# Six steps moved to other places in the first five units of a linear-attention and MLP kernel

## The chip, the cores and the metric

The kernel runs on one core of a Trainium2 chip. A time is the device time of one execution in microseconds. Its profiles come from single executions taken by the hardware profiler; a profile's span runs from the first to the last instruction. The engines are called PE (TensorE's matrix products), PEld (its weight loads, which overlap the products), DVE (VectorE), ACT (ScalarE), POOL (GpSimd) and SP (the queue that issues most DMAs).

## The reference

A linear attention with a decaying state gives y, and an MLP with SiLU follows. All data are float32.

```
B, H, S, D = 4, 8, 768, 48
for t in range(S):
    cur = einsum('bhd,bhe->bhde', u * k[t], v[t])
    y[t] = einsum('bhd,bhde->bhe', r[t], state + cur)
    state = w[t][..., None] * state + einsum('bhd,bhe->bhde', k[t], v[t])
x = y as (B*S, H*D)                  # 3072 x 384
h = x @ w_in                         # 384 x 2048
out = (h / (1 + exp(-h))) @ w_out    # 2048 x 384
```

## The kernel before

The work is cut into twelve units, 0 to 11. A unit is 128 tokens of two batches (`units` lists six stretches of tokens times two pairs of batches), so units 0 and 1 have no earlier state. A unit goes through these stages.

- `turn` brings w, k and r into a layout with the channels in the partitions (`tw`, `tk`, `tr`). For units 0 and 1 that is a product on PE with copies by ACT (L356, L357, L360), for the later ones six transposes by DVE (L336).
- Scores between tokens are made in seven levels l, doubling the block of tokens each time. `product` multiplies decays (POOL, L384). `start_keys` (L505), `odd_ones` (L495), `odd_keys` (L459) and `grow_keys` (L489, POOL) prepare the keys of a level; `grow_queries` (L471) and `prepare` (L593, L595) prepare the queries. `score_products` (L525) are the products, and `keep_masked` (L535) copies what the mask keeps into `score`. From unit 2 on two levels are computed in one `burst`.
- `bonus`, `bonus_sum` (L413, L417), `bonus_spread` and `bonus_write` (L448) put in the token's own term with u.
- `y_state` (L650) and `y` (L663) make y, copied by ACT to `yt` (L667). `turn_k` makes the keys for the state: for units 0 and 1 copies by ACT (L633) out of products of `turn_apart` (L626), later eight transposes on PE (L637) and two copies by ACT (L638). `update` (L677, L682, L691, L693) makes the new state.
- x for the MLP: `dense_x` (L701, copy L703) for units 0 and 1, DMAs (`move_x`) later.
- `up(i, m)`, m from 0 to 7: products with w_in (L754) and the SiLU by ACT (L760).
- Unit 0's output comes from `down` (L773, copied at L777). From unit 1 on it comes from seven products of half the size, `quarter(i, 0)` to `quarter(i, 6)` (L817), called q0 to q6 here. They work on sums of the activations (`sums`, L799, DVE) and of the weights (`weight_sums`, L791, DVE, four calls in the whole kernel). Their results leave PSUM by an ACT copy for q0 (L824) and by DVE additions for the others (L826). The PSUM tile `p_o` of the seven products has two buffers.

The weights come in sixteen pieces, eight of w_in and eight of w_out, and are rounded during units 0 to 2. For piece i, `head_weight` is two ACT instructions (L194, the upper part of the words, and L195), `tail_weight` one (L201, into the single PSUM tile `p_w`), `join_weight` two DVE instructions (L212, L213) and, where the staging place is used again, the DMA of a later piece; `add_weight` is a POOL addition (L225). `piece(i)` is this chain with the head and tail of piece i+1 in it.

Every engine runs its instructions in the order in which the code issues them, and that order is written by hand: the lists given to `do(...)` for units 0 to 2, and from unit 3 on `mix(i)`, which gives groups of attention steps, with `ROOM`, which says how many MLP steps (`quarter` of unit i-2, `up` of unit i-1) follow each group. `b12` and `b21` are quarters of w_out; the fourth call of `weight_sums` puts b21 - t2 in the place of b12, which q5 reads:

```
out, one, two = ((t1, b12, b11), (t2, b22, t1), (t3, b22, b12), (b12, b21, t2))[which]
left, right = ((g(0, 0), b11), (g(0, 1), b21), (s(1), t2), (s(2), t3), (s(0), t1), (g(1, 1), b12), (s(3), b22))[which]
```

Of the kernel before, what the change touches and what calls it, by code (L numbers as in the profile page):

```python
# [9 lines left out]
BF16 = mybir.dt.bfloat16  # L10
I8 = mybir.dt.int8
I32 = mybir.dt.int32
U16 = mybir.dt.uint16
U32 = mybir.dt.uint32
AF = mybir.ActivationFunctionType
# [23 lines left out]
def kernel(  # L39
# [11 lines left out]
    nc = tc.nc  # L51
# [4 lines left out]
    NL = 7  # L56
# [11 lines left out]
    NTOK = 2  # L68
# [94 lines left out]
    def staged(i):  # L163
        place = PLACES[i] - NOWN
        if place < 0:
            return own[:, PLACES[i]]
        return w_out_sb[:, 4 * place:4 * place + 4, :].rearrange("p a d -> p (a d)").bitcast(U32)
# [17 lines left out]
    shift = const.tile([128, 1], F32, name="shift")  # L185
    temps = const.tile([128, 3, 2, PW], U32, name="temps")

    def head_weight(i):
        if not rounded:
            return  # L190
        head = temps[:, 0, i % 2]

        upper = temps[:, 1, i % 2].bitcast(BF16)[:, 0:PW]
        nc.scalar.activation(out=upper, in_=staged(i).bitcast(BF16)[:, 3::4], func=AF.Abs)  # L194
        nc.scalar.activation(out=head, in_=upper.bitcast(U16), func=AF.Relu, scale=8.0 * 2.0 ** 16, bias=shift)  # L195

    def tail_weight(i):
        if not rounded:
# [60 lines left out]
    parts = sorted({(ch // 128, ch // (2 * D)) for ch in range(DM)})  # L259
# [457 lines left out]
    def both(fn, i, *args):  # L717
        return [(fn, i, b, *args) for b in range(NB)]

    def block_loads(i):  # L720
        return [(load_blocks, i, name, g) for name in "wkr" for g in range(4)]

    def mix(i):

        groups = [[*both(turn, i, "w"), (product, i, 0)],
                  [*both(turn, i, "k"), *both(turn, i, "r"), (odd_ones, i), (start_levels, i), (prepare_keys, i, 1)],
                  [(prepare, i, 1), *[(product, i, l) for l in range(1, NL)]],
                  [(burst, i, 1), (keep_level, i, 1)], [(keep_level, i, 2), (go_on, i, 2)],
                  [(prepare, i, 3), (reverse_v, i), (bonus, i, 0)],
                  [(burst, i, 3), (keep_level, i, 3), (bonus_sum, i, 0), (bonus, i, 1), (bonus, i, 2)],  # L730
                  [(keep_level, i, 4), (go_on, i, 4)],
                  [(prepare, i, 5), (bonus_sum, i, 1)] + ([(load_rk, i + 1)] if i + 1 < len(units) else []),
                  [(burst, i, 5), (keep_level, i, 5)], [(keep_level, i, 6), (go_on, i, 6), (bonus_spread, i), (bonus_write, i)],
                  both(turn_k, i), [*both(y_state, i), *both(y, i), *both(update, i), (move_x, i)]]

        loads = block_loads(i + NSLOT) if i + NSLOT < len(units) else []
        if i + 1 < len(units):
            loads.insert(len(loads) // 2, (load_values, i + 1))
        behind = groups[2:]
        for at, group in enumerate(behind):  # L740
            group += loads[at * len(loads) // len(behind):(at + 1) * len(loads) // len(behind)]
        return groups
# [89 lines left out]
    def ups(i):  # L832

        steps = [[(up, i, m)] for m in range(FC // 2)]
        for m in range(FH // 2 - 1):

            steps[FH // 2 + 1 + m].append((sums, i, m))
        steps[-1].append((sums, i, FH // 2 - 1))
        return steps

    def downs(i):
        return [[(quarter, i, x)] for x in range(7)]

    def do(*steps):
        for fn, *args in steps:
            fn(*args)
# [7 lines left out]
    def back(fn, i, *args):  # L854
        return both(fn, i, *args)[::-1]


    do((make_spread,), (beat, 16), *both(turn, 0, "k"), (odd_ones, 0), (bonus, 0, 0), (bonus, 0, 1), *both(turn, 0, "r"),
       (bonus_sum, 0, 0), (clear_dense,), (clear_state,), *back(turn, 0, "w"), (bonus, 0, 2), (start_keys, 0, nc.vector, True),
       (start_keys, 0, nc.vector, False), (grow_queries, 0, 0), (product, 0, 0, nc.vector), (odd_keys, 0, 1), (grow_keys, 0, 1),  # L860
       (make_dense,), (beat, 16))

    blocks = block_loads(2)
    others = {1: [(clear, 0), (beat, 6)], 2: [(turn, 1, 0, "r"), (head_weight, 0), (beat, 2)],
              3: [(turn, 1, 1, "r"), (head_weight, 1), (beat, 2)], 4: [(turn, 1, 1, "w"), (reverse_v, 0)],
              5: [(bonus_spread, 0), (bonus_write, 0), (turn, 1, 0, "w")], 6: [*both(turn_in, 1, "k"), *blocks[0:4], (tail_weight, 0)]}
    between = {4: [(bonus_sum, 0, 1)]}
    for l in range(1, NL):
        do((scores, 0, l, *between.get(l, ())), *[(grow_keys, 0, l + 1)] * (l + 1 < NL), *others[l])

    do((bonus, 1, 0), (bonus, 1, 1), (bonus, 1, 2), *both(y, 0), (turn_apart, 0), (join_weight, 0), (add_weight,),
       *blocks[4:8], (product, 1, 0), (tail_weight, 1), (turn_k, 0, 0), (join_weight, 1), (dense_x, 0, 0), (turn_k, 0, 1),
       *both(turn, 1, "k"), (dense_x, 0, 1), (grow_queries, 1, 0), (odd_ones, 1), (tail_weight, 2), (head_weight, 2),
       *blocks[8:12], (start_keys, 1, nc.gpsimd, True), (add_weight,), (up, 0, 0), (join_weight, 2),
       (start_keys, 1, nc.gpsimd, False), (add_weight,), (tail_weight, 3), (odd_keys, 1, 1), (head_weight, 3), (grow_keys, 1, 1),
       (scores, 1, 1, (join_weight, 3)), (add_weight,), (up, 0, 1), (tail_weight, 4), (grow_keys, 1, 2), (head_weight, 4),
# [3 lines left out]
    others = {1: [], 2: [(bonus_sum, 1, 0), (bonus_sum, 1, 1), (load_rk, 2), *both(update, 0)],  # L880
              3: [(bonus_spread, 1), (reverse_v, 1), (clear, 1), (load_values, 2)]}
# [5 lines left out]
    for m in range(1, 4):  # L887
# [1 line left out]
    do((head_weight, 8), (join_weight, 7), (scores, 1, 5), (grow_keys, 1, 6), (add_weight,), (tail_weight, 8), (up, 0, 6),  # L889
       (bonus_write, 1))  # L890

    do((scores, 1, NL - 1), (head_weight, 9), (join_weight, 8), (add_weight,), (up, 0, 7), *both(y, 1), (turn_apart, 1),
       (tail_weight, 9), *both(turn_k, 1), *both(dense_x, 1), (piece, 9), *both(update, 1), (up, 1, 0), *both(turn, 2, "w"))
    blocks = block_loads(3)

    others = {0: [(up, 1, 1), (down, 0, 0, 0), *both(turn, 2, "k"), (product, 2, 0), (product, 2, 1)],
              1: [(up, 1, 2), *both(turn, 2, "r"), *[(product, 2, l) for l in range(2, NL)], *blocks[0:3]],
              2: [(down, 0, 0, 1), (odd_ones, 2), (start_keys, 2, nc.gpsimd, True), (grow_queries, 2, 0), *blocks[3:6]],
              3: [(up, 1, 3), (start_keys, 2, nc.gpsimd, False), (reverse_v, 2), *blocks[6:9]], 4: [(level, 2, 1), (up, 1, 4), *blocks[9:12]],
              5: [(down, 0, 0, 2), (up, 1, 5), (weight_sums, 0)]}  # L900
    for m in range(6):
# [4 lines left out]
    blocks = block_loads(4)  # L906
# [2 lines left out]
    do(blocks[2], (burst, 2, 3), (keep_level, 2, 3), (keep_level, 2, 4), (go_on, 2, 4), (prepare, 2, 5), (bonus, 2, 1),  # L909
       (bonus, 2, 2), (down, 0, 1, 2), (bonus_sum, 2, 1), (load_rk, 3), (sums, 1, 1), *blocks[3:7], (down, 0, 1, 3))  # L910
    do((burst, 2, 5), (keep_level, 2, 5), (keep_level, 2, 6), (go_on, 2, 6), (up, 1, 6), (bonus_spread, 2), (bonus_write, 2),
       (load_values, 3), (weight_sums, 2), (up, 1, 7), (sums, 1, 2))
    do(*both(turn_k, 2), (sums, 1, 3), *both(y_state, 2), *both(y, 2), (weight_sums, 3), *both(update, 2), (move_x, 2),
       *blocks[7:])

    ROOM = 1, 1, 2, 1, 1, 1, 1, 1, 2, 1, 2, 1, 0
    for i in range(3, len(units)):
        steps = downs(i - 2) + ups(i - 1)
        groups = mix(i)
        for group, room in zip(groups, ROOM):  # L920
            do(*group)
            for step in steps[:room]:
                do(*step)
            steps = steps[room:]
# [32 lines left out]
```

## Time and profile before

| what | value |
|---|---|
| median of 6 runs | 652.44 us (651.54 to 653.82) |
| the profiled execution | 651.54 us, span 649.7 us |
| busy, PE / DVE / POOL / ACT | 639.9 / 431.6 / 280.9 / 203.0 us |
| time from a unit to the next from unit 3 on | 50.94 us |
| mean granted clock of TensorE | 1.00 |

A line of a list of instructions gives the start and the duration in us, the engine, the line of the code, the operation, what is written and read with shapes, and in brackets the engine's idle time ahead of it with what ended it. A line of the list of waits gives the instruction that waited, the one it waited for, the total in us, how often, and the longest.

### The profile page before, as it was taken

Reading aid. Unit: us, or ns where it says so; the run is one execution under the profiler, and the core shown is the slowest. Engines: PE = TensorE matmul, PEld = TensorE weight load, DVE = VectorE, ACT = ScalarE, POOL = GpSimd, SP = SyncE. Lnnn points to the kernel's source line nnn. Section 1 sums busy time; section 2 is a strip of 40 time slices with the busy share of each in tenths; the row PEclk is TensorE's granted clock in tenths of the full one; section 3 lists DMA queues with packets and bytes.
Section 4 is the critical chain, followed back from the end, with each engine's and each line's share of the span. In section 5 each row is a group of like instructions: output and inputs, shape, how many; then the busy total and the mean of one; then the engine's idle time right before and its main releaser. Section 6 shows DMA issues by size and latency. Waiting matters only on the chain.

```text
span 649.7 us, 12886 instructions
## 1 busy us (share of the span) xinstructions
PE 639.9 (98%) x4878; PEld 579.0 (89%) x4878; DVE 431.6 (66%) x737; ACT 203.0 (31%) x408; POOL 280.9 (43%) x356
## 2 busy tenths in 40 slices
PE   8999999989999999999999999999999999999998
PEld 7878876889899899899899899899899989989997
DVE  6979789887487576585595676576676765752031
ACT  6797971211221321331331232231232232131120
POOL 6898398455055254334425416416416505510000
PEclk9999999999999999999999999999999999999999
DMA  9956954444534414514513513433431022000000
GB/s 227 275 93 174 272 127 51 88 79 57 108 53 75 87 32 65 97 30 67 96 29 56 109 25 48 95 48 52 76 71 38 26 50 49 26 3 25 25 0 25
DMA packets 201134, 49.21 MB, mean 76 GB/s; under 512 B 188912, under 2 KB 195952, under 8 KB 201072
## 3 DMA queue, kind: packets, MB, share of 16 engines
q1 hardware_dynamic: 199488, 47.79, 36.0%
q10 hardware_dynamic: 1584, 0.59, 0.4%
q8 instruction: 39, 0.64, 0.4%
q14 instruction: 23, 0.19, 0.1%
HBM read 39.52 MB, written 4.72 MB: 68 GB/s over the span
## 4 chain that ended last, share of the span: by engine, by line
PE 88%; POOL 3%; ACT 3%; DMA 2%; SPq 2%; DVE 1%; issue 1%; DVEq 0%; POOLq 0%; ACTq 0%
PE p_h L754 35%; PE p_o L817 30%; PE p_sc L525 6%; PE p_m L525 4%; PE p_m L663 3%; PE p_m L650 2%; PE p_m L773 2%; PE p_m L348 1%; PE p_m L637 1%; SPq L106 1%; POOL tk L489 1%; PE p_sc L677 1%; DMA w_out_sb<-in_moe_w_in_dram 1%; DMA w_out_sb<-in_moe_w_out_dram 1%; ACT temps L194 1%
## 5 line engine op out<-in xcount | busy, mean ns | idle before, releaser
L754 PE MATMUL p_h<-xt,w_in_sb 128*128 128x256 f32 x1152 | 258.2, 382 | 0.7 <-ACT tk L357 0.7
L754 PEld LDWEIGHTS p_h<-xt,w_in_sb 128*128 128x128 f32 x1152 | 215.8, 190 | 32.6 <-POOL tk L505 0.9
L760 ACT ACTIVATE gt<-p_h 128x512 f32<-128x512 f32 x93 | 55.5, 597 | 225.2 <-PE p_h L754 225.1
L489 POOL TENSOR_TENSOR tk<-tk,tw 128x256 f32<-128x256 f32 x144 | 99.2, 713 | 22.4 <-ACT tk L459 16.1
L535 DVE COPY_PREDICATED score<-mask,p_sc 128x512 f32<-128x512 int8 x78 | 64.1, 884 | 60.5 <-PE p_sc L525 60.2
L817 PE MATMUL p_o<-own,temps 128*128 128x192 f32 x528 | 90.3, 328 | 2.5 <-DVE temps L826 2.5
L817 PE MATMUL p_o<-w_out_sb,gt 128*128 128x192 f32 x528 | 90.4, 328 | 0.0
L817 PEld LDWEIGHTS p_o<-own,temps 128*128 128x128 f32 x528 | 85.8, 190 | 3.9 <-DVE temps L826 2.8
L817 PEld LDWEIGHTS p_o<-w_out_sb,gt 128*128 128x128 f32 x528 | 85.9, 190 | 0.9 <-issue 0.4
L682 POOL TENSOR_TENSOR state<-state,tw 128x512 f32<-128x512 f32 x16 | 19.1, 1213 | 119.0 <-PE p_m L650 119.0
L384 POOL TENSOR_TENSOR tw<-tw 128x256 f32<-128x256 f32 (+6 forms) x83 | 38.0, 457 | 56.7 <-DVE tw L336 52.8
L799 DVE TENSOR_TENSOR temps<-gt 128x256 f32<-128x256 f32 x88 | 44.3, 503 | 21.5 <-ACT gt L760 21.5
L459 ACT COPY tk<-tk 128x256 f32<-128x256 f32 x60 | 24.6, 410 | 85.1 <-PE p_sc L525 38.1
L525 PEld LDWEIGHTS p_sc<-tr,tk 48*128 48x128 f32 x640 | 39.2, 186 | 12.7 <-issue 9.8
L471 DVE TENSOR_TENSOR tr<-tr,tw 128x512 f32<-128x512 f32 x53 | 47.3, 893 | 2.6 <-PE p_sc L525 0.8
L525 PE MATMUL p_sc<-tr,tk 48*128 48x128 f32 x640 | 47.1, 285 | 1.3 <-POOL tk L489 0.6
L406 POOL TENSOR_TENSOR ruk<-tokens_rk 128x768 f32<-128x768 f32 x10 | 18.6, 1860 | 68.7 <-DVE own_sums L413 68.7
L593 DVE TENSOR_TENSOR tr<-tr,tw 128x512 f32<-128x512 f32 x29 | 36.4, 1257 | 0.4
L535 DVE COPY_PREDICATED score<-mask,p_m 128x512 f32<-128x512 int8 x54 | 35.4, 705 | 0.0
L826 DVE TENSOR_TENSOR partial<-p_o,partial 128x192 f32<-128x192 f32 x33 | 11.7, 353 | 34.7 <-PE p_o L817 34.7
L505 POOL TENSOR_TENSOR tk<-tk,tw 128x128 f32<-128x128 f32 x44 | 32.5, 774 | 2.3 <-ACT tk L495 1.7
L817 PE MATMUL p_o<-w_out_sb,temps 128*128 128x192 f32 x176 | 30.4, 326 | 0.0
(144 smaller groups left out, 741.8 us busy)
## 6 DMA issues: line engine op xcount, KB each, us to landing
w_out_sb<-in_moe_w_in_dram SPq DMA_DIRECT2D x6, 768.0 KB, 7.3
tokens_rk<-in_r_dram SPq DMA_DIRECT2D x20, 192.0 KB, 3.3
tokens_rk<-in_k_dram SPq DMA_DIRECT2D x20, 192.0 KB, 3.7
w_out_sb<-in_moe_w_out_dram SPq DMA_DIRECT2D x4, 768.0 KB, 5.8
own<-in_moe_w_out_dram SPq DMA_DIRECT2D x4, 768.0 KB, 6.4
xt<-yt SPq DMA_DIRECT2D x60, 48.0 KB, 2.0
raw<-in_w_dram SPq DMA_DIRECT2D x80, 32.0 KB, 2.1
raw<-in_k_dram SPq DMA_DIRECT2D x80, 32.0 KB, 2.2
```

Source lines behind the costliest of these rows:

```text
L384: engine.tensor_tensor(out=up, in0=t[:, :, 0::2], in1=t[:, :, 1::2], op=ALU.mult)
L459: nc.scalar.copy(out=keys(i, X[(l + 1) % 2] * L + c, [4 * c, blocks], [c, 2], [1, c]), in_=keys(i, NP * L + c, [4 * c, blocks], [NP * L + ...
L471: nc.vector.tensor_tensor(out=odd, in0=odd, in1=tw[i][l][:, :, 0::2][:, :, :, None].to_broadcast([128, Q, L >> (l + 1), c]), op=ALU.mult)
L489: nc.gpsimd.tensor_tensor(out=out, in0=have, in1=odd_products(i, l, b, *blocks), op=ALU.mult)
L505: engine.tensor_tensor(out=keys(i, X[1] * L + 3 * b, [4, n], [1, 1]) if own else have, in0=have, in1=odd_products(i, 0, b, [4, n], skip=2 ...
L525: nc.tensor.matmul(bass.AP(tensor=s_p.tensor, offset=s_p.offset, ap=[s_p.ap[0], [apart * L // 2, 2], [1, L // 2]]), lhsT=tk[i][rows, X[l % ...
L535: nc.vector.copy_predicated(out=dst, mask=masks[l][:, :, None].to_broadcast([128, NB, NP, ni, c]), data=sc[e].rearrange("p (b q) (i c) -> ...
L593: nc.vector.tensor_tensor(out=new[:, :, :, 1, :], in0=old[:, :, :, 1, :], in1=tw[i][l][:, :, 0::2][:, :, :, None].to_broadcast([128, Q, L ...
L754: nc.tensor.matmul(p_h[:, a, :], lhsT=w_in_sb[:, c, f * 128:(f + 1) * 128], rhs=xt[i][:, c, :], start=(c == 0), stop=(c == KC - 1))
L760: nc.scalar.activation(out=gt[i, m], in_=p_h, func=AF.Silu)
L799: nc.vector.tensor_tensor(out=out, in0=one, in1=two, op=op)
L817: nc.tensor.matmul(p, lhsT=left(f), rhs=right[:, f, :], start=(f == 0), stop=(f == FH - 1))
```

## The change

Six steps are issued at another place; no instruction is added or taken out.

1. `bonus_sum(0, 1)` goes from level 4 of unit 0's scores to before `start_keys` of unit 0.
2. The key copies `turn_k(0, b)` go behind the turned keys of unit 1, `odd_ones(1)` and `tail_weight(2)`.
3. `head_weight(9)` goes from before the last `up` of unit 0 to unit 1's `dense_x`: its first instruction between the two halves, its second behind them. `tail_weight(10)` now precedes `head_weight(10)`.
4. `turn_k(2, b)` goes before the last `up` of unit 1.
5. `weight_sums(3)` goes from the end of unit 2 to the fifth group of unit 3, behind `keep_level(3, 1)`.
6. In `mix` the second group is divided: q1 with its addition now follows the transposes, and `start_levels` and `prepare_keys` come after it. This holds for units 3 to 11.

```diff
-    def head_weight(i):
+    def head_weight(i, parts=range(2)):
...
-        nc.scalar.activation(out=upper, in_=staged(i).bitcast(BF16)[:, 3::4], func=AF.Abs)
-        nc.scalar.activation(out=head, in_=upper.bitcast(U16), func=AF.Relu, scale=8.0 * 2.0 ** 16, bias=shift)
+        if 0 in parts:
+            nc.scalar.activation(out=upper, in_=staged(i).bitcast(BF16)[:, 3::4], func=AF.Abs)
+        if 1 in parts:
+            nc.scalar.activation(out=head, in_=upper.bitcast(U16), func=AF.Relu, scale=8.0 * 2.0 ** 16, bias=shift)
...
-                  [*both(turn, i, "k"), *both(turn, i, "r"), (odd_ones, i), (start_levels, i), (prepare_keys, i, 1)],
+                  [*both(turn, i, "k"), *both(turn, i, "r"), (odd_ones, i)], [(start_levels, i), (prepare_keys, i, 1)],
...
-        behind = groups[2:]
+        behind = groups[3:]
...
-       (bonus_sum, 0, 0), (clear_dense,), (clear_state,), *back(turn, 0, "w"), (bonus, 0, 2), (start_keys, 0, nc.vector, True),
+       (bonus_sum, 0, 0), (clear_dense,), (clear_state,), *back(turn, 0, "w"), (bonus, 0, 2), (bonus_sum, 0, 1), (start_keys, 0, nc.vector, True),
...
-    between = {4: [(bonus_sum, 0, 1)]}
...
-        do((scores, 0, l, *between.get(l, ())), *[(grow_keys, 0, l + 1)] * (l + 1 < NL), *others[l])
+        do((scores, 0, l), *[(grow_keys, 0, l + 1)] * (l + 1 < NL), *others[l])
...
-       *blocks[4:8], (product, 1, 0), (tail_weight, 1), (turn_k, 0, 0), (join_weight, 1), (dense_x, 0, 0), (turn_k, 0, 1),
-       *both(turn, 1, "k"), (dense_x, 0, 1), (grow_queries, 1, 0), (odd_ones, 1), (tail_weight, 2), (head_weight, 2),
+       *blocks[4:8], (product, 1, 0), (tail_weight, 1), (turn, 1, 0, "k"), (join_weight, 1), (dense_x, 0, 0), (turn, 1, 1, "k"),
+       (dense_x, 0, 1), (grow_queries, 1, 0), (odd_ones, 1), (tail_weight, 2), *both(turn_k, 0), (head_weight, 2),
...
-    do((scores, 1, NL - 1), (head_weight, 9), (join_weight, 8), (add_weight,), (up, 0, 7), *both(y, 1), (turn_apart, 1),
-       (tail_weight, 9), *both(turn_k, 1), *both(dense_x, 1), (piece, 9), *both(update, 1), (up, 1, 0), *both(turn, 2, "w"))
+    do((scores, 1, NL - 1), (join_weight, 8), (add_weight,), (up, 0, 7), *both(y, 1), (turn_apart, 1),
+       (tail_weight, 9), *both(turn_k, 1), (dense_x, 1, 0), (head_weight, 9, [0]), (dense_x, 1, 1), (head_weight, 9, [1]),
+       (join_weight, 9), (add_weight,), (tail_weight, 10), (head_weight, 10), *both(update, 1), (up, 1, 0), *both(turn, 2, "w"))
...
-       (load_values, 3), (weight_sums, 2), (up, 1, 7), (sums, 1, 2))
-    do(*both(turn_k, 2), (sums, 1, 3), *both(y_state, 2), *both(y, 2), (weight_sums, 3), *both(update, 2), (move_x, 2),
+       (load_values, 3), *both(turn_k, 2), (weight_sums, 2), (up, 1, 7), (sums, 1, 2))
+    do((sums, 1, 3), *both(y_state, 2), *both(y, 2), *both(update, 2), (move_x, 2),
...
-    ROOM = 1, 1, 2, 1, 1, 1, 1, 1, 2, 1, 2, 1, 0
+    ROOM = 1, 1, 0, 2, 1, 1, 1, 1, 1, 2, 1, 2, 1, 0
...
+        if i == NTOK + 1:
+
+            groups[4].append((weight_sums, 3))
```

## The prediction

> **What bounds the kernel now.** I read the page first (busy shares, chain), then TensorE's list of waits, then the timeline around the longest wait, then a later unit as a standard.
>
> The page's busy shares:
>
> ```profile
> PE 639.9 (98%) x4878; PEld 579.0 (89%) x4878; DVE 431.6 (66%) x737; ACT 203.0 (31%) x408; POOL 280.9 (43%) x356
> ```
>
> TensorE is the bound: it is without work for only 9.8 us of 649.7. The chain gives it 88% of the span, and the granted clock is 1.00 in every stage, so no clock is to be won. A move on another engine pays only where it ends a TensorE wait. These are its waits that lie near the moved steps (who waits, for whom: us in total, times, longest):
>
> ```profile
> PE p_o L817 <- DVE temps L826: 2.5, 1, 2.5
> ...
> PE p_h L754 <- ACT tk L357: 0.7, 1, 0.7
> ...
> PE p_sc L525 <- DVE score L535: 0.6, 1, 0.6
> PE p_m L650 <- ACT kq L638: 0.3, 1, 0.3
> PE p_m L701 <- ACT yt L667: 0.2, 1, 0.2
> ```
>
> They are all before 140 us; later TensorE is gapless up to its last product. The timeline of all engines round the first of them (start, duration, engine, line):
>
> ```profile
> 131.79 1.75 DVE L791 TENSOR_TENSOR w_out_sb<-w_out_sb,own 128x1536 f32<-128x1536 f32 x1
> ...
> 133.46 1.11 DVE L691 TENSOR_TENSOR state<-p_sc,state 48x384 f32<-48x384 f32 x2
> ...
> 134.57 2.76 PE L817 MATMUL p_o<-own,temps 128*128 128x192 f32 x16
> 134.59 1.30 DVE L336 STREAM_TRANSPOSE tw<-raw 128x512 f32<-128x512 f32 x2
> ...
> 136.97 3.00 POOL L505 TENSOR_TENSOR tk<-tk,tw 128x128 f32<-128x128 f32 x4
> ...
> 138.30 1.14 DVE L471 TENSOR_TENSOR tr<-tr,tw 128x512 f32<-128x512 f32 x1
> 139.47 0.36 DVE L826 TENSOR_TENSOR temps<-p_o,partial 128x192 f32<-128x192 f32 x1
> ...
> 139.88 2.87 PE L817 MATMUL p_o<-own,temps 128*128 128x192 f32 x16 [2.55 <-DVE temps L826]
> ...
> 140.52 1.44 POOL L489 TENSOR_TENSOR tk<-tk,tw 128x256 f32<-128x256 f32 x2 [0.55 <-ACT tk L459]
> ...
> 142.68 1.18 PE L525 MATMUL p_sc<-tr,tk 48*128 48x128 f32 x16
> ...
> 143.89 2.46 DVE L535 COPY_PREDICATED score<-mask,p_sc 128x512 f32<-128x512 int8 x2 [0.75 <-PE p_sc L525]
> ...
> 144.68 2.87 PE L817 MATMUL p_o<-own,temps 128*128 128x192 f32 x16
> ```
>
> Call the seven products of a unit's output q0 to q6. They alternate between two PSUM buffers, so q3 (139.88) needs q1's buffer. q1 ends at about 134.7, but L826, which empties it, stands on VectorE behind L791, L691, six L336 and L471 and runs at 139.47. q2 ends at 137.33: hence 2.55 us. The same place one unit later:
>
> ```profile
> 188.32 5.36 PE L817 MATMUL p_o<-own,temps 128*128 128x192 f32 x32
> 189.07 1.16 DVE L471 TENSOR_TENSOR tr<-tr,tw 128x512 f32<-128x512 f32 x1
> 190.26 0.36 DVE L826 TENSOR_TENSOR temps<-p_o,partial 128x192 f32<-128x192 f32 x1
> ...
> 193.62 0.98 PEld L525 LDWEIGHTS p_sc<-tr,tk 48*128 48x128 f32 x16 [0.23 <-POOL tw L384]
> ```
>
> There q2 and q3 run as one group of 32: no subtraction of weights stands in the way, and nothing is to be won.
>
> **The change part by part.** No moved step issues a DMA, and the order on SP and on POOL stays as it is. The joins that trigger weight loads (pieces 12 to 15) keep their places on SP.
>
> *Unit 0's sums.* Two reductions (1.00 us for both at 23.00) go to the end of L408 (10.29), in front of L505. VectorE stands idle there for 1.16 us, waiting for ScalarE's tw copy, which ends at 11.41. They end near 11.25: 0 us, with 0.15 to spare; L505 is on the chain, so what they exceed counts in full. At 23 us nothing is won, since TensorE has no gap from 16.06 to 31. Bounds: 0 to +0.2.
>
> *Unit 0's key copies.* Four L633 (two of 0.54 us each time) leave 33.38 and 34.62 for a place behind the third L201. The turned keys of unit 1 and L201 come 0.9 us sooner, but TensorE's next wait (0.74 at 36.30) is in truth for the second xt copy on VectorE (35.59 to 36.15, just ahead of it), which starts when dense_x ends: it stays. Behind it ScalarE loses some 0.2 us of idle time in front of L703, so L194, L760 and the next L201 (40.04) come 0.13 sooner. L201, L212, L213, L471, L535 is the chain to the wait of 0.62 at 46.65. I take 0.1 (bounds 0 to 0.3; L201 also needs L760, which needs the product ending at 39.1). The copies hold both p_sc buffers until about 37.6, and scores need them at 39.05: covered by 1.4 us.
>
> *Upper parts of weights 9.* L194 and L195 (0.93 + 0.94 at 68.09) stood before L760 and the yt copies. Without them yt starts when its product is done (69.5, not 70.57) and dense_x follows turn_apart at once: 0.2 gained. L194 now lies between the two xt copies: from about 72.9 to 73.8, while dense_x's second half ends at 73.8. The second xt ends at 74.4, and TensorE is at the state's products until 74.6: covered by 0.2. Bounds: +0.4 to -0.2. L195 moves from 69.11 to some 74.3, POOL's addition from 74.61 to 75.4. POOL's next addition is at 79.68 and piece 9 is first read near 80.9: hidden. L760 of unit 1 may slip by some tenths, which ScalarE's idle 1.39 us at 85.59 takes up.
>
> *Turned keys of unit 2.* Eight L637 go between two products of `up`. ScalarE's copies (1.07) then run beside the second (2.7 us), so L650 does not wait: 0.3 gained. The copies come ahead of L760, whose output is read by the last L799 at 130: hidden.
>
> *Fourth subtraction and grouping.* Without L791, L691 starts at 131.5 instead of 133.46, counting the 0.6 us won before. Six transposes and L826 follow; from L691 to the end of the transposes is 4.84 in the trace, so L826 ends at 136.7. q2 ends at 137.33 - 0.6 = 136.7: all 2.55 go. What is late next? The burst at 139.5 needs the keys: 6.0 us after the first transposes (L384 1.04, four L505 3.00, ScalarE 0.55, L489 1.44), so 139.7, and its second half needs them at 140.6. Covered by 0.9.
>
> The new wait is q5, which reads the weights that L791 now makes behind L535. L535 starts 1.2 after the burst, at 140.7, lasts 2.4, and L791 starts at 143.1. q4 ends at 144.2. With 1.75 us L791 ends at 144.85 and q5 waits 0.7. Queued behind L791 on VectorE are q4's two L826 (needed by q6, 147.6), L535 and L471: covered by 1.5.
>
> *A rule against it.* The other long subtraction with POOL's key products beside it took 2.22 us, the three without 1.75. Two L799 beside POOL's L682 took 1.26 and 1.15 instead of 0.41. The Trainium skill (SBUF — State Buffer, Who interferes with whom) says that a VectorE instruction with two SBUF inputs and a GpSimd instruction that reads SBUF exclude each other, and the second waits for the first to finish. At 131.79 POOL was idle; at 143.1 its four L489 (2.62) are running, then L404 (1.00). By the lowest row the loss at q5 is 0.7, by the 2.22 row 1.15, by the rule with a whole L404 in front 1.7. I take 0.9: the L489 are nearly done by then.
>
> *Units 4 to 11.* L826 goes ahead of L471. q1 is done when VectorE gets there (188.5 against 189.0), so L471 starts 0.36 later. L593, which follows, ends at 191.3 and the burst is at 193.62: covered by 2. 0 us.
>
> The other rule weighed is how to measure the gap. TensorE's matmul row says 2.55, its weight-load row 2.8. The skill (Perfetto Trace Analysis, Identifying the Most-Contended Engine) calls matmul busy time a poor measure of headroom and prefers weight-load time. The sum would be 0.25 better; I keep the smaller, since the products start by the first.
>
> **Sum:** 0 + 0.1 + 0.2 + 0.3 + 2.55 - 0.9 + 0 = 2.25 us gained. The profiled execution took 651.54 (span 649.7), the lowest of six; it becomes 649.3, the span 647.4. Off the median of 652.44: 650.2.
>
> **The rivals.**
> 1. *The exclusion at q5 is longer, or the head's tenths do not come.* With q5 at 1.7 and the head at 0: 2.55 + 0.3 - 1.7 = 1.15, so 651.3. For it: L404 follows just there.
> 2. *The burst waits for the keys instead.* POOL's L505 run beside the transposes and L471. If the 6.0 us become 8, the burst's second half comes 1.1 late: 651.3. With 3.2 us or more nothing is left: 652.4. Against it: unit 4 shows the same spacing (L384 186.74 to L489 191.33).
> 3. *Slower: L826 ahead of L471 in units 4 to 11.* If the burst hung on L471, the 0.36 would be paid in eight units: 2.9 lost against 2.25 won, 653.1. It decides from 0.28 per unit; at 0.44, which takes a wait for q1 as well, the kernel is slower beyond the measurement. For it: the weight load there ends an idle 0.23. Against: the 2 us of cover.
> 4. *The wait is not L826's.* q3 also reads sums and weights of VectorE, but these end at 131.9. Then 652 or so.
>
> **How the numbers follow.** The forecast (gain 1.5 to 2.6) 0.72; rival 1 0.12; rival 2 0.08; rival 3 0.05; rival 4 0.03. A measurement of this kernel can tell about 0.2%, 1.3 us, from no change. Faster by more: the forecast, half of rival 1 and a little of 2: 0.80. Slower: 0.05, rounded up to 0.06 for what I do not see; the rest, 0.14, is within. The forecast alone is 649.8 to 650.9; the runs scatter by 2.3, so a median is good to half a microsecond. Reaching to rivals 1 and 2: 649.2 to 651.6.
>
> **What would show it.** Right: q2 and q3 as one L817 group of 32 near 134; one wait of 0.6 to 1.2 for L791 at q5 near 145; L650 and L701 gone from the list of waits; L791 near 143 with 1.75 to 2.2 us; TensorE's idle time down from 9.8 to about 7.5; units from 150 us on alike and 50.94 apart. Wrong: a q5 wait over 2, a burst near 140 waiting for POOL, L505 of unit 0 after 11.6, or gaps in units 4 to 11.

## The result, and the profile after

| | before | after |
|---|---|---|
| median | 653.17 us (37 runs, 650.59 to 658.76) | 650.25 us (16 runs, 648.71 to 651.34) |
| profiled execution / its span | 651.54 / 649.7 us | 650.52 / 648.7 us |
| TensorE idle in the span | 9.8 us | 648.7 - 639.4 = 9.3 us |

The ratio of the times is 0.9952, with a 95% interval from 0.9936 to 0.9968: about 3.1 us faster (2.1 to 4.2), where 2.25 was forecast. Line numbers of after are those of before plus 2 (the subtraction is L793, the addition that empties q1 is L828). The page's busy shares:

```profile
PE 639.4 (99%) x4878; PEld 578.3 (89%) x4878; DVE 433.4 (67%) x737; ACT 203.6 (31%) x408; POOL 282.6 (44%) x356
```

TensorE has the same work, and its granted clock is 1.00 again. Its list of waits in after (who waits, for whom: us in total, times, longest), without those below 0.25:

```profile
PE p_m L854 <- POOL ident masks.py:199: 1.4, 1, 1.4
PE p_m L665 <- ACT score L556: 0.9, 1, 0.9
PE p_o L819 <- DVE w_out_sb L793: 0.8, 1, 0.8
PE p_h L756 <- POOL tk L507: 0.7, 1, 0.7
PE p_sc L527 <- POOL tk L491: 0.6, 1, 0.6
PE p_m L350 <- DMA raw<-in_k_dram: 0.4, 1, 0.4
PE p_h L527 <- DVE tr L473: 0.4, 1, 0.4
PE p_o L819 <- DVE temps L828: 0.4, 1, 0.4
PE p_h L756 <- ACT gt L762: 0.3, 1, 0.3
```

Gone are the 2.5 us for q1's addition (0.4 is left), the 0.6 for `score`, and those of L650 and L701. New are 0.8 for the moved subtraction, as forecast, and four that the prediction did not have: 0.9 for L556, 0.4 for L473, 0.3 for L762, and 0.4 for the DMA of an input block at 5 us, ahead of every moved step. The timeline of all engines around q3 and q5 (start, duration, engine, line, and in brackets the idle time ahead with its releaser):

```profile
134.15 2.76 PE L819 MATMUL p_o<-own,temps 128*128 128x192 f32 x16
...
136.88 0.36 DVE L828 TENSOR_TENSOR temps<-p_o,partial 128x192 f32<-128x192 f32 x1
137.15 0.87 DVE L473 TENSOR_TENSOR tr<-tr,tw 128x512 f32<-128x512 f32 x1
137.29 2.87 PE L819 MATMUL p_o<-own,temps 128*128 128x192 f32 x16 [0.38 <-DVE temps L828]
...
141.30 2.46 DVE L537 COPY_PREDICATED score<-mask,p_sc 128x512 f32<-128x512 int8 x2 [0.75 <-PE p_sc L527]
...
142.83 4.01 POOL L491 TENSOR_TENSOR tk<-tk,tw 128x256 f32<-128x256 f32 x4
143.56 2.17 DVE L793 TENSOR_TENSOR w_out_sb<-w_out_sb,own 128x1536 f32<-128x1536 f32 x1
...
145.79 2.87 PE L819 MATMUL p_o<-w_out_sb,gt 128*128 128x192 f32 x16 [0.84 <-DVE w_out_sb L793]
```

q3 starts at 137.29 instead of 139.88, q5 waits 0.84, and the unit's next burst starts at 151.19 instead of 152.67. Followed along the span, after leads before by 0.31 us at unit 2's state products (L652 at 124.37, L650 at 124.68), by 2.59 at q3, by 1.48 at that burst, and by only 0.93 at unit 4's q2 (187.39 against 188.32). From 152 us to the end TensorE has one gap, and it is where the last half microsecond goes. The row's gap is 0.28, but the starts show the whole cost: from the transposes (L639) to the state products (L652) after takes 177.60 - 173.59 = 4.01 us, before 178.54 - 175.07 = 3.47.

```profile
169.84 2.44 SPq L425 DMA_DIRECT2D diag<-own_sums  x4
172.29 0.20 ACT L441 COPY both_b<-diag 128x16 f32<-128x16 f32 x1 [3.08 <-DMA diag<-own_sums]
...
173.53 0.84 ACT L443 COPY both_b<-diag 32x16 f32<-32x16 f32 x4 [1.03 <-DMA diag<-own_sums]
...
174.27 1.06 ACT L762 ACTIVATE gt<-p_h 128x512 f32<-128x512 f32 x2
174.91 2.86 PE L756 MATMUL p_h<-xt,w_in_sb 128*128 128x256 f32 x12 [0.28 <-ACT gt L762]
```

The four DMAs of the diagonal stand in SP's queue behind the block loads of a later unit. In before they were issued at 169.44, when the products were 1.48 us later, and TensorE waited for nothing. In after they come at 169.84 although TensorE is early; ScalarE stands at L441 and L443 for them, with the SiLU (L762) queued behind, and TensorE waits for that. The next experiments test this.

### The profile page after: what moved, and what is told of

The parts are those of the page before. It is cut to its first block, busy times and chain, and to the rows that moved or that the text cites. A ratio compares the mean times of both kernels' runs of the same rounds, so it can differ in the third digit from the quotient of the medians.

```text
span 648.7 us, 12887 instructions
## 1 busy us (share of the span) xinstructions
PE 639.4 (99%) x4878; PEld 578.3 (89%) x4878; DVE 433.4 (67%) x737; ACT 203.6 (31%) x408; POOL 282.6 (44%) x356
## 4 chain that ended last, share of the span: by engine, by line
PE 87%; DVE 4%; DMA 3%; SPq 3%; ACT 1%; issue 1%; POOL 0%; DVEq 0%; ACTq 0%; POOLq 0%
PE p_h L756 33%; PE p_o L819 31%; PE p_sc L527 6%; PE p_m L527 3%; PE p_m L775 3%; PE p_m L665 3%; PE p_m L652 3%; SPq L106 2%; PE p_m L639 1%; DVE score L537 1%; DMA u_bc<-in_u_dram 1%; PE p_m L350 1%; DMA w_out_sb<-in_moe_w_in_dram 1%; PE p_sc L679 1%; DMA w_out_sb<-in_moe_w_out_dram 1%
## 5 line engine op out<-in xcount | busy, mean ns | idle before, releaser
L762 ACT ACTIVATE gt<-p_h 128x512 f32<-128x512 f32 x93 | 55.4, 596 | 223.6 <-PE p_h L756 223.4
L491 POOL TENSOR_TENSOR tk<-tk,tw 128x256 f32<-128x256 f32 x144 | 103.3, 741 | 21.7 <-ACT tk L461 15.1
L684 POOL TENSOR_TENSOR state<-state,tw 128x512 f32<-128x512 f32 x16 | 19.3, 1227 | 119.0 <-PE p_m L652 119.0
L801 DVE TENSOR_TENSOR temps<-gt 128x256 f32<-128x256 f32 x88 | 44.3, 503 | 21.5 <-ACT gt L762 21.5
L473 DVE TENSOR_TENSOR tr<-tr,tw 128x512 f32<-128x512 f32 x53 | 46.1, 870 | 3.3 <-POOL tk L491 1.1
L408 POOL TENSOR_TENSOR ruk<-tokens_rk 128x768 f32<-128x768 f32 x10 | 18.6, 1859 | 66.7 <-DVE own_sums L415 66.7
L595 DVE TENSOR_TENSOR tr<-tr,tw 128x512 f32<-128x512 f32 x29 | 39.3, 1354 | 1.3
L597 ACT COPY tr<-tr 128x512 f32<-128x512 f32 x29 | 18.4, 635 | 37.2 <-DVE tr L473 36.4
L507 POOL TENSOR_TENSOR tk<-tk,tw 128x128 f32<-128x128 f32 x44 | 29.3, 701 | 1.7 <-ACT tk L497 1.7
## 6 DMA issues: line engine op xcount, KB each, us to landing
tokens_rk<-in_r_dram SPq DMA_DIRECT2D x20, 192.0 KB, 3.4
tokens_rk<-in_k_dram SPq DMA_DIRECT2D x20, 192.0 KB, 3.8
```

What stands on the lines that cost most here:

```text
L473: nc.vector.tensor_tensor(out=odd, in0=odd, in1=tw[i][l][:, :, 0::2][:, :, :, None].to_broadcast([128, Q, L >> (l + 1), c]), op=ALU.mult)
L491: nc.gpsimd.tensor_tensor(out=out, in0=have, in1=odd_products(i, l, b, *blocks), op=ALU.mult)
L507: engine.tensor_tensor(out=keys(i, X[1] * L + 3 * b, [4, n], [1, 1]) if own else have, in0=have, in1=odd_products(i, 0, b, [4, n], skip=2 ...
L595: nc.vector.tensor_tensor(out=new[:, :, :, 1, :], in0=old[:, :, :, 1, :], in1=tw[i][l][:, :, 0::2][:, :, :, None].to_broadcast([128, Q, L ...
L762: nc.scalar.activation(out=gt[i, m], in_=p_h, func=AF.Silu)
L801: nc.vector.tensor_tensor(out=out, in0=one, in1=two, op=op)
```

## The experiments

Times are medians; each ratio is to runs of before on the same chip (653.15 in the first group, 653.84 in the second). The last group was run once each (650.00, 653.52, 653.89 and 650.49 us in the order below, before beside them 654.05) and is read by its traces alone.

**First group: which part does what near q3.**

Parts 5 and 6 alone, put on before:

```diff
-    do(*both(turn_k, 2), (sums, 1, 3), *both(y_state, 2), *both(y, 2), (weight_sums, 3), *both(update, 2), (move_x, 2),
+    do(*both(turn_k, 2), (sums, 1, 3), *both(y_state, 2), *both(y, 2), *both(update, 2), (move_x, 2),
...
+        if i == NTOK + 1:
+            groups[4].append((weight_sums, 3))
```

with the second group of `mix` divided as in the change.

> Before with the moves of the fourth subtraction and the grouping alone (parts 5 and 6). Theory: the unit 3 exchange carries the gain, 2.55 us of wait at q3 against some 0.9 at q5: 1.5 to 1.9 us faster than before in time, and in the trace q3's wait falls to under 0.6 while q5 gets one of 0.7 to 1.2. The wait of 0.62 for L535 near 46.65 and that of 0.29 at L650 stay. Rival (the gain sits in the head: the tail of the other four moves makes most of the measured 0.48%): under 0.7 us faster.

Measured: 651.54, ratio 0.9976 (0.9953 to 0.9998), about 1.6 us (0.1 to 3.1). q2 and q3 run as one group of 32, and q5 pays what it pays in after:

```profile
135.39 5.36 PE L817 MATMUL p_o<-own,temps 128*128 128x192 f32 x32
...
144.16 2.17 DVE L791 TENSOR_TENSOR w_out_sb<-w_out_sb,own 128x1536 f32<-128x1536 f32 x1
...
146.38 2.87 PE L817 MATMUL p_o<-w_out_sb,gt 128*128 128x192 f32 x16 [0.83 <-DVE w_out_sb L791]
```

So these two parts end q3's wait without the others. The waits of before at 46.7 (0.62) and 125.5 (0.29) are still there, and that of L701 is 0.89. TensorE also waits 0.66 for the SiLU at 175.9: part of the gain is given back there too.

Parts 1 to 4 alone:

```diff
-    ROOM = 1, 1, 0, 2, 1, 1, 1, 1, 1, 2, 1, 2, 1, 0
+    ROOM = 1, 1, 2, 1, 1, 1, 1, 1, 2, 1, 2, 1, 0
...
-            groups[4].append((weight_sums, 3))
```

with the fourth subtraction and `mix` as in before.

> Before with parts 1 to 4 alone (sums, key copies, weights 9, turned keys). Theory: 0.3 at L650 and 0.6 at the scores near 46, and 0.2 at dense_x: 0.6 to 1.2 us faster than before; the wait of 2.5 at q3 stays as it is. Rival: these moves are worth 1.5 us or more because they also take up the late landing of the weights near 64 us. The forecast had 0.6 for the four.

Measured: 652.74, ratio 0.9988 (0.9963 to 1.0014), not told from no change. The waits at 46, L652 and L703 are gone, but one line shows where their gain went:

```profile
138.96 0.36 DVE L828 TENSOR_TENSOR temps<-p_o,partial 128x192 f32<-128x192 f32 x1
139.37 4.55 PE L819 MATMUL p_o<-own,temps 128*128 128x192 f32 x16 [3.22 <-DVE temps L828]
```

q3's wait has grown from 2.55 to 3.22, where it was expected to stay. The group ahead of q3 starts 1.19 us earlier than in before (133.38 against 134.57), VectorE's addition and q3 only 0.51 earlier (139.37 against 139.88): more than half of what the head won ends in this wait.

The second line holds something else. q3's sixteen products take 4.55 us, where they took 2.87 in before. TensorE's granted clock was halved behind the wait. By stretches of 1 us (the stretch, its length, TensorE's busy time and products, the granted clock, the DMA share, GB/s):

```profile
138.00:139.00 1.00, 0.00 (x0) 1.00 0.17 43
...
141.00:142.00 1.00, 1.00 (x4) 0.50 0.27 73
...
144.00:145.00 1.00, 1.00 (x20) 1.00 0.42 51
```

This one stretch costs 4.55 - 2.87 = 1.7 us. What it does to the medians is told at the end of this group.

After with the division of the group undone (part 6), and after with the subtraction put back (part 5):

```diff
-                  [*both(turn, i, "k"), *both(turn, i, "r"), (odd_ones, i)], [(start_levels, i), (prepare_keys, i, 1)],
+                  [*both(turn, i, "k"), *both(turn, i, "r"), (odd_ones, i), (start_levels, i), (prepare_keys, i, 1)],
```

> After, with the division of the second group taken back (part 6 undone), so that L826 of q1 stands behind L471 again in all units. Theory: q3 of unit 3 waits 1.2 to 1.6 us instead of 0.38, q5's wait is the same as before within 0.3, units 4 to 11 stay without a wait: about 1.0 us slower than after. Rival (the grouping is not needed once the subtraction is gone): no difference from after.

```diff
-    do((sums, 1, 3), *both(y_state, 2), *both(y, 2), *both(update, 2), (move_x, 2),
+    do((sums, 1, 3), *both(y_state, 2), *both(y, 2), (weight_sums, 3), *both(update, 2), (move_x, 2),
...
-            groups[4].append((weight_sums, 3))
```

> After, with the fourth subtraction back at the end of unit 2 (part 5 undone). Theory: L826 of q1 runs 1.7 us later, q3 waits 1.8 to 2.2 us, q5 waits for nothing: about 0.9 us slower than after. Rival (the grouping alone does it, the subtraction only brings a new wait): as fast as after or faster, q3's wait under 0.8.

Measured: 651.77, ratio 0.9974 (0.9951 to 0.9996), and 651.16, ratio 0.9962 (0.9932 to 0.9992). With the head's parts in, the four traces give q3's wait for every combination:

| q3 waits (us) | group whole | group divided |
|---|---|---|
| subtraction in unit 2 | 3.22 | 2.03 |
| subtraction in unit 3 | 1.65 | 0.38 |

The division takes 1.19 or 1.27, the move of the subtraction 1.57 or 1.65, each whatever the other does. The division takes L471 out of the way: 1.15 us in the trace of the undivided group (L473 at 137.60, ahead of L828 at 138.78). There unit 4's q3 waits 0.70 at 192.0 as well, where no wait was expected. Without the moved subtraction there is no wait at q5 and none at 175. Its median is the lowest of this group's four, but the intervals overlap.

**What the waits do to the clock.** The trace with the subtraction put back shows the same halving behind q3's wait of 2.03 (0.50 from 139 to 141, and again 4.55 us for q3's products), and the trace of the third group with the turned keys put back shows it behind a wait of 1.92 for L556. Not every long wait brings it: the profile of before has 2.55 us at q3 and a clock of 1.00. One halved stretch lowers the mean clock of an execution to 0.997 (1.7 of 650 us is 0.26%), so the clocks on record show how often it happens:

| first group | executions at 0.997 or lower |
|---|---|
| before | 18 of 35 |
| parts 1 to 4 alone | 9 of 12 |
| after with the subtraction put back | 4 of 10 |
| parts 5 and 6 alone | 0 of 12 |
| after with the group undivided | 0 of 10 |

After itself has none in 17. In the second group before has 11 of 16, and the four kernels tested there, all with the subtraction in unit 3, none in 29. So moving the subtraction also ends most of the halvings, which the prediction had ruled out as a gain because the one profile of before showed a clock of 1.00. The 17 executions of before at 1.00 in the first group have a median of 652.41, against 653.15 for all 35. By that mark some 0.7 us of a gain measured against before is clock, and of the 1.6 us of parts 5 and 6 alone 0.9 remain. These are estimates between medians. No trace of before with a lowered clock was kept, so it is not shown that its halvings lie at q3 too.

**Second group: what is late next, and can it be taken away.** The subtraction ahead of both copies of `keep_level(3, 1)` instead of behind them:

```diff
-            groups[4].append((weight_sums, 3))
+            groups[4].insert(1, (weight_sums, 3))
```

> After, with the fourth subtraction one step earlier on VectorE: behind the burst of unit 3 but ahead of keep_level(3, 1). Theory (q5's wait is only the place of the subtraction): it runs near 140.6 while VectorE would wait for the burst, ends near 142.5, and q5's wait of 0.84 is gone. But the diagonal's DMA of unit 3 lands at an hour of its own, near 172, so the wait for L762 near 175 grows by what q5 gives: less than 0.4 us faster than after. Rival (the wait near 175 follows TensorE): 0.8 faster, no larger wait near 175.

Measured: 651.15, ratio 0.9953 (0.9932 to 0.9974). q5's wait is gone, and the ratio is no better than after's 0.9952. From q3 to the next burst TensorE takes 12.80 us instead of 13.90, so 1.1 are won at q5. ScalarE and TensorE 30 us later:

```profile
170.34 2.44 SPq L425 DMA_DIRECT2D diag<-own_sums  x4
172.78 0.20 ACT L441 COPY both_b<-diag 128x16 f32<-128x16 f32 x1 [4.19 <-DMA diag<-own_sums]
...
175.39 2.86 PE L756 MATMUL p_h<-xt,w_in_sb 128*128 128x256 f32 x12 [1.39 <-ACT gt L762]
```

The wait for the SiLU is 1.39 instead of 0.28, and the way from L639 to L652 takes 5.12 us instead of 4.01: the 1.1 won at q5 are given back at the diagonal's DMAs. (This run is 0.5 us later than after's throughout, by a wait of 1.41 instead of 0.92 for L556 at 69, of which below; 175.39 against 174.91 is just that.) If that is so, the same kernel must gain once SP is free at that time. Hence after with the block loads of unit 3 (and of it alone) from the eleventh group on, so that the diagonal goes first:

```diff
-        behind = groups[3:]
+        behind = groups[10:] if i == NTOK + 1 else groups[3:]
```

> After, with unit 3's block loads (for unit 5) moved on SP behind the diagonal's DMAs: in unit 3 alone they follow the groups from the tenth on. Theory (the wait near 175 is SP's: the diagonal's issues stand behind the loads): the diagonal is issued near 160 and not 169.8, ScalarE no longer waits for it, the wait of 0.28 near 175 is gone and TensorE there follows at once: 0.3 to 0.6 us faster than after. Rival (the wait near 175 is an accident of one profile, or the diagonal waits for VectorE's sums): no difference from after, diagonal issued near 170.

Measured: 649.55 (6 runs, 649.13 to 650.51), ratio 0.9937 (0.9913 to 0.9961), by the ratios 1.0 us better than after, where 0.3 to 0.6 were expected; the intervals overlap. The diagonal's DMAs are issued at 158.43, ScalarE's copies wait for nothing, and TensorE has no gap there:

```profile
168.26 0.20 ACT L441 COPY both_b<-diag 128x16 f32<-128x16 f32 x1
168.47 0.84 ACT L443 COPY both_b<-diag 32x16 f32<-32x16 f32 x4
...
173.62 2.75 PE L756 MATMUL p_h<-xt,w_in_sb 128*128 128x256 f32 x12
```

Both edits together:

> After, with both: the subtraction ahead of keep_level(3, 1) and unit 3's block loads behind the diagonal's DMAs. Theory: q5's wait and the wait near 175 are both gone and nothing gives the gain back: 1.1 to 1.5 us faster than after. Rival (the gain is given back at another wait in unit 3 or 4): under 0.6 us faster, with a new wait on TensorE in the list.

Measured: 648.71 (6 runs, 647.87 to 649.49), ratio 0.9922 (0.9898 to 0.9946), 2.0 us better than after where 1.1 to 1.5 were expected. Neither q5 nor 175 waits; what is left, besides waits that before has too, is 0.38 at q3 and 1.03 for L556. So the give-back is shown from both sides: the subtraction's earlier place alone brings no measurable gain, and with SP's loads later the median falls by 0.84 with it. The intervals of these two overlap; the waits in the traces are the firmer evidence.

The 1.03 for L556 has another cause, which the scatter of the runs shares. In after, SP's queue and ScalarE show it:

```profile
49.55 9.80 SPq L106 DMA_DIRECT2D raw<-in_r_dram  x16
59.88 1.77 SPq L178 DMA_DIRECT2D w_out_sb<-in_moe_w_out_dram  x2
```

```profile
65.31 0.91 ACT L195 ACTIVATE temps<-w_out_sb 128x768 bf16<-128x768 bf16 x1 [3.29 <-DMA w_out_sb<-in_moe_w_out_dram]
...
68.41 0.75 ACT L556 COPY score<-p_sc 64x256 f32<-64x256 f32 x2
...
68.82 1.09 PE L665 MATMUL p_m<-score,vt 128*64 128x128 f32 x16 [0.92 <-ACT score L556]
```

Weight pieces 8 and 9 are issued behind sixteen block loads (0.61 us each here, 0.54 in before's trace). ScalarE waits for piece 8 with L195, and `score` (L556), which has nothing to do with it, stands four instructions further back. L195 starts between 64.0 and 66.9 in the thirteen traces that have this order; where it starts after about 64.9, unit 1's y waits (1.03 at 64.98, 0.92 at 65.31, 1.76 at 65.97, 1.92 at 65.96, all with part 3). So the two pieces were loaded ahead of the block loads, on top of the two edits:

```diff
-       *blocks[8:12], (start_keys, 1, nc.gpsimd, True), (add_weight,), (up, 0, 0), (join_weight, 2),
+       (start_keys, 1, nc.gpsimd, True), (add_weight,), (up, 0, 0), (join_weight, 2),
...
-       (scores, 1, 1, (join_weight, 3)), (add_weight,), (up, 0, 1), (tail_weight, 4), (grow_keys, 1, 2), (head_weight, 4),
+       (scores, 1, 1, (join_weight, 3)), *blocks[8:12], (add_weight,), (up, 0, 1), (tail_weight, 4), (grow_keys, 1, 2), (head_weight, 4),
```

> As the kernel with both, and on SP the loads of weight pieces 8 and 9 ahead of the r blocks of unit 2 instead of behind them. Theory (the time at which piece 8 lands, 64.0 to 66.0 in the profiles so far, makes the wait for L556 near 69 and the scatter of the runs): piece 8 lands before 62, ScalarE does not wait for it, TensorE has no wait near 69 or 71, and the kernel is 0 to 1.2 us faster than the one with both, with less scatter. Rival (another transfer, the r blocks or pieces 10 and 11, becomes late): as fast or slower, with a wait at L338 or for a later piece.

Measured: 648.02 (6 runs, 647.74 to 648.52), ratio 0.9912 (0.9889 to 0.9935), 5.8 us less than before and the lowest of all; the intervals of this and of the version without the reordering overlap. Of the 5.8 a part is before's clock: its four executions at 1.00 in this group have a median of 651.87, 3.9 us above this kernel. The pieces are issued at 50.67, L195 waits for no DMA, and y for no `score`:

```profile
61.98 0.92 ACT L195 ACTIVATE temps<-w_out_sb 128x768 bf16<-128x768 bf16 x1
...
65.19 0.76 ACT L556 COPY score<-p_sc 64x256 f32<-64x256 f32 x2
...
67.88 1.09 PE L665 MATMUL p_m<-score,vt 128*64 128x128 f32 x16
```

Six runs lie within 0.8 us; those of the two edits alone within 1.6, and sixteen of after within 2.6. That the landing of piece 8 makes most of the scatter agrees with this; with unequal numbers of runs it is not proved.

**Third group: each part of the head undone alone in after.** Key copies back in their old place:

```diff
-       *blocks[4:8], (product, 1, 0), (tail_weight, 1), (turn, 1, 0, "k"), (join_weight, 1), (dense_x, 0, 0), (turn, 1, 1, "k"),
-       (dense_x, 0, 1), (grow_queries, 1, 0), (odd_ones, 1), (tail_weight, 2), *both(turn_k, 0), (head_weight, 2),
+       *blocks[4:8], (product, 1, 0), (tail_weight, 1), (turn_k, 0, 0), (join_weight, 1), (dense_x, 0, 0), (turn_k, 0, 1),
+       *both(turn, 1, "k"), (dense_x, 0, 1), (grow_queries, 1, 0), (odd_ones, 1), (tail_weight, 2), (head_weight, 2),
```

> After, with unit 0's key copies back in front (part 2 undone). Theory: the wait of 0.6 near 46 comes back, because POOL's first key product of unit 1 (L491) again runs at 42.1 beside L473 and L473 takes 1.2 us instead of 0.74; the copies' own order on ScalarE moves L203 by 0.1 only. Rival (the forecast: the chain through L203 alone, worth 0.1): the wait near 46 is 0.1 in size, L473 stays at 0.74.

The wait of 0.62 is back, at 46.32. First this kernel, then after, at the same step (this execution runs 0.34 us ahead of after's from the first scores on, 13.10 against 13.44):

```profile
41.79 1.44 POOL L491 TENSOR_TENSOR tk<-tk,tw 128x256 f32<-128x256 f32 x2
42.56 1.22 DVE L473 TENSOR_TENSOR tr<-tr,tw 128x512 f32<-128x512 f32 x1
43.70 2.47 DVE L537 COPY_PREDICATED score<-mask,p_sc 128x512 f32<-128x512 int8 x2
```

```profile
41.53 1.45 POOL L491 TENSOR_TENSOR tk<-tk,tw 128x256 f32<-128x256 f32 x2
42.79 0.74 DVE L473 TENSOR_TENSOR tr<-tr,tw 128x512 f32<-128x512 f32 x1
43.45 2.48 DVE L537 COPY_PREDICATED score<-mask,p_sc 128x512 f32<-128x512 int8 x2
```

In after POOL's two products end 0.19 after L473 starts, in the other 0.67 after. L473 takes 0.74 there and 1.22 here: the time saved is that of one instruction which no longer runs into POOL's.

The upper parts of weights 9 back:

```diff
-    do((scores, 1, NL - 1), (join_weight, 8), (add_weight,), (up, 0, 7), *both(y, 1), (turn_apart, 1),
-       (tail_weight, 9), *both(turn_k, 1), (dense_x, 1, 0), (head_weight, 9, [0]), (dense_x, 1, 1), (head_weight, 9, [1]),
-       (join_weight, 9), (add_weight,), (tail_weight, 10), (head_weight, 10), *both(update, 1), (up, 1, 0), *both(turn, 2, "w"))
+    do((scores, 1, NL - 1), (head_weight, 9), (join_weight, 8), (add_weight,), (up, 0, 7), *both(y, 1), (turn_apart, 1),
+       (tail_weight, 9), *both(turn_k, 1), *both(dense_x, 1), (piece, 9), *both(update, 1), (up, 1, 0), *both(turn, 2, "w"))
```

> After, with the head of piece 9 back in front of the last up of unit 0 (part 3 undone). Theory: L703's wait for L669 at dense_x comes back, 0.2 if piece 8 lands near 64.2 and 0.9 if it lands near 65, as in the kernel with unit 3's parts alone; with a landing after 65.5 a wait for L556 ahead of it as well. Rival (the head of piece 9 is hidden anyway): no wait at L703 however late the piece lands.

Piece 8 was late in this run (L195 at 66.89), and both costs show: 1.90 for L556 and, behind it, 0.88 for `yt`, which no trace with part 3 shows:

```profile
PE p_m L665 <- ACT score L556: 1.9, 1, 1.9
...
PE p_m L703 <- ACT yt L669: 0.9, 1, 0.9
```

The turned keys of unit 2 back:

```diff
-       (load_values, 3), *both(turn_k, 2), (weight_sums, 2), (up, 1, 7), (sums, 1, 2))
-    do((sums, 1, 3), *both(y_state, 2), *both(y, 2), *both(update, 2), (move_x, 2),
+       (load_values, 3), (weight_sums, 2), (up, 1, 7), (sums, 1, 2))
+    do(*both(turn_k, 2), (sums, 1, 3), *both(y_state, 2), *both(y, 2), *both(update, 2), (move_x, 2),
```

> After, with unit 2's turned keys back behind the last up of unit 1 (part 4 undone). Theory: the wait of 0.29 at L652 comes back, and the start of q0 behind the state products comes 0.4 us later against the start of the last up; q3 then waits less or not at all, because VectorE's L828 keeps its time. Rival (the copies are hidden): no wait at L652.

L652 waits its 0.29 again, and q3 waits for nothing. This kernel first, then after, at unit 2's state products:

```profile
127.01 2.05 PE L652 MATMUL p_m<-tr,state 128*128 128x128 f32 x16 [0.29 <-ACT kq L640]
127.96 1.75 DVE L793 TENSOR_TENSOR own<-w_out_sb 128x1536 f32<-128x1536 f32 x1
```

```profile
124.37 1.95 PE L652 MATMUL p_m<-tr,state 128*128 128x128 f32 x16
125.51 3.74 POOL L684 TENSOR_TENSOR state<-state,tw 128x512 f32<-128x512 f32 x2 [7.17 <-PE p_m L652]
125.77 2.58 DVE L793 TENSOR_TENSOR own<-w_out_sb 128x1536 f32<-128x1536 f32 x1
```

With the products earlier, POOL's L684 starts 0.26 ahead of the third subtraction instead of 0.29 behind it (128.25), and the subtraction takes 2.58 instead of 1.75. That is not yet q3's wait, for one of the sums behind it, L801, then takes 0.42 where it takes 1.15 in this run: from the subtraction's start to the third sum it is 4.14 us in after and 4.03 here, 0.11 more. The larger part is that VectorE did not take part in TensorE's gain. Counted from L652, the subtraction starts 1.40 later in after, but 0.95 in this run and in before; ahead of it VectorE is busy without a gap, and its L450 starts at 123.38 in after, its counterpart L448 at 123.23 in before. Together L828 is 0.56 later against L652, of which this run had 0.19 to spare. That gives q3's 0.38. A late start of the whole execution is not the reason: the run with the upper parts of weights 9 back is as late, and its q3 waits 0.37.

The sums of unit 0 back:

```diff
-       (bonus_sum, 0, 0), (clear_dense,), (clear_state,), *back(turn, 0, "w"), (bonus, 0, 2), (bonus_sum, 0, 1), (start_keys, 0, nc.vector, True),
+       (bonus_sum, 0, 0), (clear_dense,), (clear_state,), *back(turn, 0, "w"), (bonus, 0, 2), (start_keys, 0, nc.vector, True),
...
-        do((scores, 0, l), *[(grow_keys, 0, l + 1)] * (l + 1 < NL), *others[l])
+        do((scores, 0, l, *between.get(l, ())), *[(grow_keys, 0, l + 1)] * (l + 1 < NL), *others[l])
```

> After, with unit 0's two sums back at level 4 of its scores (part 1 undone). Theory: no wait of TensorE changes between 13 and 36 us beyond 0.1; L507 of unit 0 on VectorE starts as soon as the tw copy is there in both. Rival (the sums ahead of L507 make it late, which is what the wait of 0.4 for L473 near 13.4 in the profile of after shows): that wait is gone here and the scores of unit 1 start 0.3 us earlier.

No wait for L473 near 13. But the data landed later in this run (L507 starts at 11.97), so it does not give the price. Of the eleven traces that hold the moved sums, four (after, the two edits of the second group each alone, and the weights put back) show a wait for L473 of 0.36 to 0.84, the others none.

## Why the prediction was right, point by point

- **q3's wait** (all of 2.55 to go): it shrank by 2.17, to 0.38, and in the run of parts 5 and 6 alone it vanished. The term and its reason stand; the two-by-two table shows that both edits were needed. The 0.38 comes from the start of L691, forecast at 131.5 and found at 132.04 (L693); from there to L826 it took the 4.84 of the forecast. The working let VectorE start 0.3 earlier with TensorE, and it started 0.25 later than the 131.79 at which the subtraction had stood.
- **The wait at q5** (0.9, bounds 0.7 to 1.7): 0.84. L793 took 2.17 at 143.56, where 143.1 was forecast; the choice near the 2.22 row was right in size. Its reason was not: the key products were not nearly done. Of the four L491 (starts 142.83, 143.46, 144.20 and 146.2) the second had just begun at 143.56. VectorE waited for that one alone, and the third then waited for VectorE. The L404 was not met.
- **Units 4 to 11** (0): TensorE has no gap there. With the group whole and the subtraction moved, unit 4 waits 0.70.
- **Key copies** (0.1, bounds 0 to 0.3): mis-sized. The wait at 46.65 went altogether, 0.6. The prediction followed ScalarE's chain to L471 and took L471's 1.24 us as its price. L471 itself did start about 0.1 earlier (42.79 against 42.87). But POOL's chain moved by 0.58 (41.53 against 42.11), and L473, no longer beside POOL's products, takes 0.74 instead of 1.24.
- **Turned keys** (0.3): TensorE gains it at L652 and pays 0.38 at q3. The term was costed alone. Its consequence two steps behind was not looked for: VectorE's queue keeps its own time, and POOL's state product now meets the third subtraction with a lead of 0.26.
- **Weights 9** (0.2, bounds +0.4 to -0.2): the wait of 0.2 went; where piece 8 lands late, that wait is 0.9 without the move (parts 5 and 6 alone, and the weights put back). The trace of before happened to show an early landing.
- **Sums** (0, bounds 0 to +0.2): 0 in most traces, 0.4 to 0.8 in some. In after, L408's counterpart (L410) waited 0.40 for u's DMA, and the two reductions (1.01) behind it ended after the copy that L507 needs. (The pair of profiles hides this: the products start at 13.44 in after and 13.43 in before, where that copy came later.) The cover of 0.15 was read from one execution, and the landing of a DMA varies by more.
- **Units from 150 us on alike**: wrong. The lead shrinks from 1.48 to 0.93 near 175, since SP's queue did not move with TensorE. TensorE's idle time is 9.3, not 7.5: 0.92 for piece 8, 0.41 for the sums, 0.41 for an input block, 0.38 at q3 and 0.28 at 175 are 2.4 more, the better key copies 0.5 less, together 9.4.
- **No clock to be won**: wrong outside the one profile. In over half of before's executions with a clock on record (29 of 51) it is lower, which no term of the sum has.

That the median is so near, 650.25 against 650.2, is partly luck. The forecast takes 2.25 off the median of six runs, 652.44; over 37 runs before's median is 653.17. The gain is larger than forecast by about as much, 3.1, and the two cancel. The likeliest source of both is the clock: before's executions at 1.00 have a median of 652.41, from which after is 2.2 away, close to the forecast. This fits but is not proved, since the clocks of those 37 runs are not on record. A late piece 8, which makes part 3 worth more, can add to it. How much each adds stays open, since parts 5 and 6 alone (1.6) and parts 1 to 4 alone (0.8) have intervals of over a microsecond on either side. The two profiled executions differ by only 1.02, where 2.25 was forecast; before's had piece 8 at 64.21, among the early ones, and after's at 65.31, and after's also met the late data of the sums.

## What to carry to other kernels

When a release on an in-order queue is made earlier, follow the gained time to the next instructions that keep their own hour, DMA queues above all: here 1.1 us won at q5 came back as 1.1 us at a transfer issued behind loads that nobody needed yet. A wait on TensorE can cost more than its length: behind three waits of 1.9 to 3.2 us the clock was halved, which cost some 1.7 us more (4.55 against 2.87 where q3 shows it), in some executions and not in others, so the clocks of many executions say more than one profile. Cover of a few tenths is to be weighed against how much a DMA's landing varies between executions, which one profile cannot show. And where VectorE reads two SBUF operands, look up what POOL is doing at its start: a shift of half a microsecond changed its duration by about half or more (0.74 to 1.22 us, 1.75 to 2.58).

## What the runs showed of the hardware

The slowing of VectorE and POOL beside each other looks like an exclusion that is handed over after each single instruction. The Trainium skill (SBUF — State Buffer, Who interferes with whom) says that a VectorE instruction with two SBUF inputs contends with a GpSimd one that reads SBUF, and that issue order decides who is blocked. POOL's four L491 in after, as the view of that line gives them (ns, min/median/max), and L489 in before, alone:

```profile
L491 POOL TENSOR_TENSOR tk<-tk,tw x4: 638/670/2036, 142.8 to 146.2; 128x256 f32<-128x256 f32 x4
```

```profile
L489 POOL TENSOR_TENSOR tk<-tk,tw x4: 644/656/668, 144.5 to 146.5; 128x256 f32<-128x256 f32 x4
```

Three keep their 0.65, and one takes 2.04. That agrees with an alternation: L793 waits for the L491 that is running (2.17 - 1.75 = 0.42), then one L491 waits for L793 (2.04 - 0.65 = 1.4), while POOL's row loses 1.39 in all. The third subtraction fits too. In after it starts behind L684 and takes 0.83 longer, less than the 0.97 left of a first L684 of 1.23. In the run with the turned keys put back it starts ahead, takes its 1.75, and the first L684 takes 2.35. In these traces the price to VectorE stays within what is left of one POOL instruction, whatever stands in the queue behind it. If that holds, the prediction's upper end, a whole L404 in front, needed L404 running at that moment; no run here tried it.
